# The opening work list of a local-convolution and maxout kernel, written anew

## The chip, the cores and the metric

The kernel runs on one core of one Trainium2 chip. The metric is the device time of one execution in microseconds (us). Engines are named as the profile names them: PE is TensorE, DVE VectorE, ACT ScalarE, POOL GpSimd, SP SyncE.

## The reference, cut to what matters

Each of 33280 positions (8 sequences of 4160) has 192 channels in 8 heads of 24. A softmax over 7 weights for each position and head mixes the position with the six before it. The result goes through three up matrices, an elementwise maximum of the three, and a down matrix.

```python
w = exp(weight_gen - max(weight_gen)); w = w / (sum(w) + 1e-9)   # over the 7 taps
x = einsum('bshk,bskhg->bshg', w, x_unf)                         # 7 taps, 8 heads of 24 channels
h = np.maximum(np.maximum(x @ w1, x @ w2), x @ w3)               # 192 -> 768
return (h @ w_out).astype(np.float32)                            # 768 -> 192
```

The up and down matrices come in as float64.

## The kernel before, in words

The positions are cut into 65 chunks of 512 (four tiles of 128). Chunk 0 is loaded alone, the later ones three at a time (a *super*: 0 is chunk 0, 1 is chunks 1 to 3, 2 is chunks 4 to 6). For each chunk the kernel does this:

- **softmax** (`softmax`, L207, once for a super, name `s`): a maximum over the taps on DVE (L212), a subtraction on POOL (L214), exp on ACT (L219), sum, addition and reciprocal on DVE (L221 to L223), a multiplication on POOL (L226).
- **products and sums** (`product`, L231, name `x<chunk>.<tile>`; `total`, L254, name `+`): POOL multiplies a tile's seven taps by the weights (L243), DVE adds the seven up (L258).
- **transpose** (`transpose`, L263, name `t`): channels onto partitions. For chunks 0 to 2 that is PE's work, two matmuls a tile into two PSUM tiles (L273, L274); later ones go through DVE's block transpose (L281) and 24 small copies on ACT (L287).
- **parts** (`parts`, L290, name `p`): the transposed values are split into a high and a low fp32r part: `xa_hi` on ACT (L297), `xa_lo` on DVE (POOL for chunk 3 and on, L301), `xc` and `xb` on ACT (L303, L305) and the lower half of `xb` on DVE or POOL (L306).
- **up** (`up`, L340): nine steps `(chunk, jp, i)`, where `jp` is a pair of 128-column blocks and `i` one of the three matrices. A step fills two PSUM tiles with nine matmuls for the upper and nine for the lower half of PE's rows; the second half of a step runs beside the first half of the next. `maximum` (L357) drains a tile: for `i = 0` a copy on ACT (L373), else a maximum on DVE (L375). After `i = 2` ACT rounds the result to `h_hi` (L378) and POOL makes `h_lo` (L382).
- **down** (`down`, L386): four groups of 24 matmuls, one a tile, drained by ACT (L405) and DVE (L406). Chunk c's stand in the middle of chunk c + 1, behind its sixth up step.

In the opening the weights have to be split too, from float64 words into fp32r high and low parts (`split`, L442). There are nine pieces `a0` to `a8`, one for each up step (step k of chunk 0 needs `a<k>`), three pieces `b0` to `b2` (one for every three steps) and six pieces `d0` to `d5` of the down matrix, all of which are needed before the down step of chunk 0. One piece has four stages: an absolute value on ACT (L458); a triple on DVE (L460, L462, L467); a rounding on ACT (L472) with a second triple on DVE (L474, L479, L483); and a scaling on ACT (L485) with a product on POOL (L486), which is the low part. A `b` piece has four more copies on ACT (L541). A piece holds one PSUM tile (a `b` piece two) from its first stage to its last.

All eight PSUM banks are one pool, named `ph`, for splits, transposes, up and down. Each engine takes its instructions in the order in which the program wrote them.

That order is written by ticks. A chunk has 22: two for an up step, four for the down groups. `OPENING` (L26) gives, for the first chunks, the stages written at each tick; each name there writes the next stage of that piece of work. `stage` (L569) first finishes what the named work needs: a `p` finishes its chunk's whole transpose, a `t` the sums, a sum its product. Work that `OPENING` doesn't name is written at the fixed ticks of `PRODUCTS`, `SUMS`, `TRANSPOSE`, `PARTS` and `SOFTMAX` (L85 to L89). The loop at L624 writes a tick's listed work ahead of that tick's matmuls; at the start of a chunk it finishes that chunk's `p`, and in chunk 0 the `a` and `b` of the step (L637 to L641), wherever the list has put them.

Of the kernel before, what the change touches and what calls it, by code (L numbers as in the profile page):

```python
# [24 lines left out]

OPENING = {  # L26
    -1: (
        "x0.0 s0 s0 x0.1 a0 a0 a0 a0 x0.2 +0.0 s0 x0.3 a2 a2 b0 +0.1 a1 b0 +0.2 b0 a3 a1 "
        "+0.3 s1 b0 a1 a2 s1 a1 s1 b0 a4 a2"
    ),  # L30
    0: "a6 b1 a6 a3 t0",
    1: "a6 a3 a5 a6 b1",
    2: "t0",
    3: "t0 a4 t0 a3 b1",
    4: "a5",
    5: "x1.0",
    6: "p0 b2 +1.0 x1.1",
    7: "s0 x1.2 a4 s1",
    8: "+1.1 t1",
    9: "a5 b2 a5 x1.3 b1",  # L40
    10: "b2 p0",
    11: "+1.2 b2 a4",
    12: "+1.3",
    13: "b1",
    15: "t1",
    16: "p0 a7 a8 a7 p1",
    17: "a7 d1",
    18: "t1 s2 a7 d1 a8",
    19: "p1 b2 a8",
    20: "d2 d2 d1",  # L50
    21: "d0",
    22: "d0",
    23: "d0",
    24: "+2.0 t1",
    25: "d2 +2.1 d1 p1",
    26: "d0 d3 d5",
    27: "d2 x2.1 d3",
    28: "d3 x2.2",
    29: "x2.0 x2.3 d3 d4 a8",
    31: "d4 s2 +2.2",  # L60
    32: "d5 d4 d5",
    33: "t2 +2.3 t2 t2",
    35: "d4 x3.2 p2",
    38: "p2 d5 p2 x3.0",
    42: "x3.1",
    43: "t3 t3",
    46: "t2 t3 +3.3 s2 +3.1 s2",
    48: "+3.2 +3.0",
    52: "x4.1 t3",
    56: "x4.0 p3",  # L70
    57: "p3 x3.3",
    59: "+4.1",
    60: "t3",
    61: "x4.2",
    66: "t3 x4.3",
    70: "t3",
    71: "p3",
    72: "+4.3 +4.2",
    74: "+4.0",
}  # L80


# [602 lines left out]
```

## Time and profile before

| | |
|---|---|
| time, median of 3 runs | 1723.65 us (1722.03 to 1723.68) |
| the profiled execution's time | 1720.92 us |
| its span, first to last instruction | 1719.1 us |
| mean granted TensorE clock | 0.996 |

Busy time of the span: PE 97%, POOL 83%, DVE 66%, ACT 66%. From the sixth chunk on, the first matmul of each chunk follows that of the chunk before by 25.35 us. The profile's line of 40 slices shows PE full from the third slice to the last but one.

Times in the views are us from the start of the span. A row of the timeline is: start, duration, engine, line, operation, output<-inputs, count, and in square brackets the engine's idle time just before it with what ended it. DVE's successive instructions overlap by some 0.1 us, so what one costs the queue is the distance to the next start.

### The profile page before, as it was taken

The page shows a single profiled execution, that of the slowest core. Times are in us where ns is not written, and L with a number is a line of the kernel's source. Part 1 is how long each engine was busy: PE and PEld are TensorE (multiplying, and loading weights), DVE is VectorE, ACT ScalarE, POOL GpSimd, SP SyncE. Part 2 cuts the span into 40 slices and gives each one's busy share as a digit, 9 for nine tenths or more (in the row PEclk, how much of TensorE's full clock was granted, in tenths as well). Part 3 has the DMA queues.
Part 4 walks back from the last instruction along what each step waited for, and adds up shares of the span by engine and source line. Part 5 has one row for each costly group of instructions (what it writes and reads, how often), then busy time and mean ns, then how long its engine had stood idle before and what let it go on. Part 6 is the DMA issues. An engine that isn't in the chain of part 4 may idle for free.

```text
span 1719.1 us, 42111 instructions
## 1 busy us (share of the span) xinstructions
PE 1671.4 (97%) x16794; PEld 1642.6 (96%) x16794; DVE 1136.5 (66%) x1570; ACT 1138.8 (66%) x2878; POOL 1427.9 (83%) x844
## 2 busy tenths in 40 slices
PE   2799999999999999999999999999999999999998
PEld 1589999999999999999999999999999999999998
DVE  7967666666666666666666666666666666666653
ACT  4556667667667667766766766766676676676662
POOL 5888888988888898888888898988889888888862
PEclk9999999999999999999999999999999999999999
DMA  7010101101010110101010110101011010101000
GB/s 233 1 69 10 69 20 60 69 20 59 20 70 10 69 48 32 69 20 69 11 70 20 60 69 19 60 20 69 17 63 69 20 60 20 69 11 45 20 11 29
DMA packets 19989, 79.50 MB, mean 46 GB/s; under 512 B 2272, under 2 KB 4568, under 8 KB 17104
## 3 DMA queue, kind: packets, MB, share of 16 engines
q1 hardware_dynamic: 19672, 76.54, 11.8%
q8 instruction: 131, 2.15, 0.5%
q14 instruction: 66, 0.54, 0.1%
q10 hardware_dynamic: 120, 0.28, 0.1%
HBM read 51.25 MB, written 25.56 MB: 45 GB/s over the span
## 4 chain that ended last, share of the span: by engine, by line
PE 92%; DVE 3%; POOL 2%; DMA 2%; issue 1%; SPq 0%; ACT 0%; POOLq 0%; ACTq 0%; DVEq 0%
PE ph L326 92%; DMA xt<-in_x_dram 1%; POOL r L243 1%; DVE acc L258 1%; DVE m L375 1%; POOL h_lo L382 1%; DMA h_lo<-in_moe_w_dram 0%; DVE e L483 0%; DVE ph L479 0%; DVE ph L462 0%; DVE ph L467 0%; DVE ph L474 0%; DVE ph L460 0%; POOL wt L226 0%; ACT wb_hi L541 0%
## 5 line engine op out<-in xcount | busy, mean ns | idle before, releaser
L243 POOL TENSOR_TENSOR r<-xt,wt 128x1344 f32<-128x1344 f32 x260 | 722.0, 2819 | 0.6 <-DMA h_hi<-in_moe_w_dram 0.6
L375 DVE TENSOR_TENSOR m<-ph,m 128x512 f32<-128x512 f32 x780 | 523.2, 685 | 217.9 <-PE ph L326 119.5
L382 POOL TENSOR_TENSOR h_lo<-m,h_hi 128x512 fp32r<-128x512 f32 x390 | 504.0, 1304 | 163.7 <-ACT h_hi L378 158.8
L326 PE MATMUL ph<-xa_hi,wa_hi 64*128 64x512 f32 x2340 | 626.8, 390 | 11.3 <-ACT xa_hi L297 4.4
L326 PE MATMUL ph<-xa_lo,wa_hi 64*128 64x512 f32 x2340 | 623.9, 388 | 2.8 <-DVE xa_lo L301 2.8
L326 PE MATMUL ph<-xa_hi,wa_lo 64*128 64x512 f32 x2340 | 623.3, 388 | 1.4 <-POOL wa_lo L486 1.3
L326 PE MATMUL ph<-xb,wb_hi 64*128 64x512 f32 x2340 | 623.0, 387 | 0.2 <-POOL xb L306 0.2
L326 PE MATMUL ph<-wo,h_hi 64*128 64x384 f32 x3120 | 597.0, 358 | 0.0
L326 PE MATMUL ph<-wo,h_lo 64*128 64x192 f32 x3120 | 554.9, 250 | 1.6 <-POOL h_lo L382 1.6
L378 ACT CAST h_hi<-m 128x512 fp32r<-128x512 f32 x390 | 241.9, 621 | 401.6 <-DVE m L375 398.6
L326 PEld LDWEIGHTS ph<-wo,h_hi 64*128 64x128 f32 x3120 | 486.1, 185 | 7.4 <-SPq L335 0.3
L326 PEld LDWEIGHTS ph<-wo,h_lo 64*128 64x128 f32 x3120 | 484.5, 188 | 2.2 <-POOL h_lo L382 2.1
L258 DVE TENSOR_REDUCE acc<-r 128x192 f32<-128x1344 f32 x260 | 401.9, 1547 | 109.1 <-POOL r L243 109.1
L287 ACT COPY room<-room 32x128 f32<-32x128 f32 x1488 | 440.7, 296 | 26.1 <-DVE room L281 7.9
L326 PE MATMUL ph<-xc,wb_lo 64*128 64x512 f32 x1170 | 453.2, 387 | 1.2 <-POOL wb_lo L486 1.2
L326 PEld LDWEIGHTS ph<-xa_hi,wa_hi 64*128 64x128 f32 x2340 | 364.2, 185 | 19.1 <-ACT m L373 5.9
L326 PEld LDWEIGHTS ph<-xa_hi,wa_lo 64*128 64x128 f32 x2340 | 357.5, 185 | 5.1 <-POOL wa_lo L486 3.0
L326 PEld LDWEIGHTS ph<-xa_lo,wa_hi 64*128 64x128 f32 x2340 | 357.0, 185 | 4.8 <-DVE xa_lo L301 3.3
L326 PEld LDWEIGHTS ph<-xb,wb_hi 64*128 64x128 f32 x2340 | 357.7, 185 | 2.8 <-POOL xb L306 0.7
L373 ACT COPY m<-ph 128x512 f32<-128x512 f32 x390 | 221.8, 585 | 56.3 <-PE ph L326 46.9
L406 DVE TENSOR_TENSOR o<-ph,ob 128x192 f32<-128x192 f32 x260 | 86.7, 353 | 240.4 <-ACT ob L405 240.4
L326 PEld LDWEIGHTS ph<-xc,wb_lo 64*128 64x128 f32 x1170 | 216.1, 185 | 3.0 <-POOL wb_lo L486 1.6
(57 smaller groups left out, 700.0 us busy)
## 6 DMA issues: line engine op xcount, KB each, us to landing
xt<-in_x_dram SPq DMA_DIRECT2D x20, 1728.0 KB, 7.0
out_dram<-o SPq DMA_DIRECT2D x65, 384.0 KB, 2.3
wt<-in_weight_gen_dram SPq DMA_DIRECT2D x21, 336.0 KB, 3.0
h_hi<-in_moe_w_dram SPq DMA_DIRECT2D x6, 256.0 KB, 5.0
xt<-in_x_dram SPq DMA_DIRECT2D x1, 1536.0 KB, 9.0
h_lo<-in_moe_w_dram SPq DMA_DIRECT2D x6, 192.0 KB, 5.5
room<-in_moe_w_out_dram SPq DMA_DIRECT2D x1, 1152.0 KB, 8.0
xt<-in_x_dram SPq DMA_DIRECT2D x1, 960.0 KB, 5.7
```

Source lines behind the costliest of these rows:

```text
L243: nc.gpsimd.tensor_tensor(r.rearrange("p (h g) k -> p k h g", g=G), xt[:, la + t : la + t + K].rearrange("p k (h g) -> p k h g", g=G), wt[ ...
L258: nc.vector.tensor_reduce(state["acc", c][:, t], r, axis=AX.X, op=ALU.add)
L287: pin(nc.scalar.copy(to[:, :, p : p + 32], blocks[p : p + 32, :, f : f + 32]))
L326: ins = nc.tensor.matmul(ph[:, :n], w[h], v[h], start=half == 0 and q == 0, stop=half == 1 and q == len(terms) - 1,)
L373: pin(nc.scalar.copy(m[:, :N], ph[:, :N]))
L375: pin(nc.vector.tensor_tensor(m[:, :N], ph[:, :N], m[:, :N], op=ALU.max))
L378: later(1, lambda: pin(nc.scalar.copy(hi, m[:, :N])))
L382: nc.gpsimd.tensor_tensor(lo, m[:, :N], hi.bitcast(F32), op=ALU.subtract)
L406: pin(nc.vector.tensor_tensor(o[:, t], po[:, :D], ob, op=ALU.add))
```

## The change: the diff

The list `OPENING` is replaced, and nothing else. Both lists lead to the same instructions on the same tiles; their order along each engine differs.

```diff
@@ -25,58 +25,59 @@
 
 OPENING = {
     -1: (
-        "x0.0 s0 s0 x0.1 a0 a0 a0 a0 x0.2 +0.0 s0 x0.3 a2 a2 b0 +0.1 a1 b0 +0.2 b0 a3 a1 "
-        "+0.3 s1 b0 a1 a2 s1 a1 s1 b0 a4 a2"
+        "s0 s0 s0 s0 x0.0 a0 a0 +0.0 a0 x0.1 x0.2 +0.1 a1 b0 x0.3 a1 b0 b0 +0.2 b0 p0 a2 "
+        "+0.3 s1 p0 a2 t0"
     ),
-    0: "a6 b1 a6 a3 t0",
-    1: "a6 a3 a5 a6 b1",
-    2: "t0",
-    3: "t0 a4 t0 a3 b1",
-    4: "a5",
-    5: "x1.0",
-    6: "p0 b2 +1.0 x1.1",
-    7: "s0 x1.2 a4 s1",
-    8: "+1.1 t1",
-    9: "a5 b2 a5 x1.3 b1",
-    10: "b2 p0",
-    11: "+1.2 b2 a4",
-    12: "+1.3",
-    13: "b1",
-    15: "t1",
-    16: "p0 a7 a8 a7 p1",
-    17: "a7 d1",
-    18: "t1 s2 a7 d1 a8",
-    19: "p1 b2 a8",
-    20: "d2 d2 d1",
-    21: "d0",
-    22: "d0",
-    23: "d0",
-    24: "+2.0 t1",
-    25: "d2 +2.1 d1 p1",
-    26: "d0 d3 d5",
-    27: "d2 x2.1 d3",
-    28: "d3 x2.2",
-    29: "x2.0 x2.3 d3 d4 a8",
-    31: "d4 s2 +2.2",
-    32: "d5 d4 d5",
-    33: "t2 +2.3 t2 t2",
-    35: "d4 x3.2 p2",
-    38: "p2 d5 p2 x3.0",
-    42: "x3.1",
-    43: "t3 t3",
-    46: "t2 t3 +3.3 s2 +3.1 s2",
-    48: "+3.2 +3.0",
-    52: "x4.1 t3",
-    56: "x4.0 p3",
-    57: "p3 x3.3",
+    0: "b0 a1 a3 t0 a3 t0",
+    2: "b1",
+    3: "a2 s1 a3 t0 b1",
+    4: "a1 a3 p0",
+    5: "b1 a5 a5 a2 s1 a6",
+    7: "a5 a4 b2 s1 x1.0 a4",
+    8: "a0 b1 a5 a4 b2 a4",
+    9: "a6 b2",
+    10: "x1.1 a6",
+    11: "a7 b2 a7 +1.1 a7 +1.0 a7 d0",
+    12: "b2 a8",
+    15: "a6 x1.2",
+    16: "a8 b1 x1.3",
+    18: "t1 d0",
+    19: "a8 a8 +1.2",
+    21: "+1.3 d0 d1 d1 x2.0 d3 t1 t1 p1 p1 d1 x2.1 d2 d2",
+    22: "d1 d0",
+    23: "p1 d4 d2",
+    24: "d2 d5",
+    25: "t1 d3 x2.2 d5",
+    27: "d4",
+    28: "d3 d5",
+    29: "d4 d3 +2.2 d5",
+    30: "d4",
+    31: "x2.3",
+    34: "+2.3",
+    36: "+2.1 p2 x3.1 t2 x3.0 s2 t2 t2 +2.0 t2 p2",
+    40: "+3.0",
+    41: "x3.2 +3.1",
+    46: "+3.2",
+    47: "+3.3",
+    48: "t3 s2",
+    50: "t3 s2 t3 p2",
+    51: "s2 x4.0",
+    55: "t3",
+    56: "+4.0 t3 t3",
+    57: "x3.3 x4.1 t3",
     59: "+4.1",
-    60: "t3",
-    61: "x4.2",
-    66: "t3 x4.3",
-    70: "t3",
-    71: "p3",
-    72: "+4.3 +4.2",
-    74: "+4.0",
+    61: "p3",
+    62: "p3",
+    63: "x4.2",
+    68: "+4.2",
+    69: "t4",
+    70: "p3 +4.3",
+    73: "t4 t4",
+    74: "t4",
+    78: "p4",
+    79: "t4",
+    80: "t4",
+    81: "p4 x4.3 p4 t4",
 }
```

Some of what it comes to, counted along both lists:

- Chunk 0's parts `p0`, and with them its transposes, are written ahead of `a2`, `a3`, `s1` and `b1` where before they stood behind the first triples of `a3` and `a6` and behind the sums of `s1`. `a0`'s scaling on ACT comes behind `p0`.
- `a6` goes from ticks 0 and 1 to ticks 5 to 15, `a4` and `a5` to ticks 5 to 8; `a7` comes at tick 11 instead of 16, `d0` at 11 to 21.
- Chunk 1's sums go from ticks 6 to 12 to ticks 11 to 21, its transposes from ticks 8 to 16 to ticks 18 to 21.
- Of chunk 2's sums, `+2.0` and `+2.1` go from ticks 24 and 25 to tick 36, behind the maxima of chunk 1's sixth step, with the softmax maximum of `s2`. All of chunk 2's transposes are written at tick 36, between the second and the third down group of chunk 0; before, three tiles' were written at tick 33 and the last at tick 35, ahead of the second group.
- Chunk 3's four sums, all at tick 43 before, are at ticks 40, 41, 46 and 47, and its transpose and parts some five ticks later. `p3`'s second POOL instruction comes ahead of the product `x4.3` instead of behind it.

## Rows read from the trace of the kernel before

**Rows 1.** The page, part 1: busy us of each engine over the span.
```profile
PE 1671.4 (97%) x16794; PEld 1642.6 (96%) x16794; DVE 1136.5 (66%) x1570; ACT 1138.8 (66%) x2878; POOL 1427.9 (83%) x844
```

**Rows 2.** Busy time by stretch; the first line names the columns.
```profile
core 0: us, PE busy (x) PEld busy (x) DVE busy (x) ACT busy (x) POOL busy (x), PEclk, DMA share, GB/s
24.00:60.00 36.00, 22.65 (x119) 14.22 (x119) 34.63 (x65) 19.71 (x45) 22.97 (x17) 0.97 0.31 114
60.00:91.00 31.00, 25.27 (x189) 18.20 (x190) 29.76 (x63) 15.12 (x37) 26.22 (x20) 0.93 0.00 1
88.03:101.68 13.65, 13.65 (x155) 13.14 (x152) 9.69 (x15) 6.07 (x13) 13.01 (x8) 1.00 0.01 2
101.68:154.32 52.64, 52.08 (x520) 47.11 (x517) 36.10 (x49) 35.29 (x89) 41.79 (x25) 1.00 0.15 57
300.00:400.00 100.00, 100.00 (x1017) 99.57 (x1014) 66.37 (x89) 67.67 (x174) 87.67 (x51) 1.00 0.10 39
```

**Rows 3.** Waits of PE from 24 to 140: total us, times, longest.
```profile
PE ph L326 <- ACT xa_hi L297: 4.4, 1, 4.4
PE ph L326 <- ACT m L373: 4.1, 3, 2.0
PE ph L273 <- DVE acc L258: 3.1, 3, 1.6
PE ph L326 <- ACT f L485: 1.7, 3, 0.9
```

**Rows 4.** Timeline of DVE, 13 to 25: a triple, sums and a softmax maximum.
```profile
13.23 0.42 DVE L460 TENSOR_SCALAR ph<-ph 128x256 f32<-128x256 f32 x1
...
14.50 1.54 DVE L258 TENSOR_REDUCE acc<-r 128x192 f32<-128x1344 f32 x1
17.08 0.57 DVE L460 TENSOR_SCALAR ph<-ph 128x384 f32<-128x384 f32 x1 [1.03 <-ACT ph L458]
...
23.00 1.55 DVE L258 TENSOR_REDUCE acc<-r 128x192 f32<-128x1344 f32 x1
24.46 0.84 DVE L212 TENSOR_REDUCE red<-wt 128x96 f32<-128x672 f32 x1
```

**Rows 5.** Timeline of DVE, 60 to 61 and 86 to 95.
```profile
60.71 0.84 DVE L212 TENSOR_REDUCE red<-wt 128x96 f32<-128x672 f32 x1
...
88.13 1.54 DVE L258 TENSOR_REDUCE acc<-r 128x192 f32<-128x1344 f32 x1
89.59 2.47 DVE L375 TENSOR_TENSOR m<-ph,m 128x512 f32<-128x512 f32 x4
```

**Rows 6.** Timeline of PE: last transposes, first matmuls, a wait, the third down group.
```profile
24.60 0.48 PE L273 MATMUL ph<-ident,acc 128*128 128x128 f32 x1 [1.12 <-DVE acc L258]
...
29.70 0.79 PE L326 MATMUL ph<-xa_hi,wa_hi 64*128 64x512 f32 x1 [4.41 <-ACT xa_hi L297]
33.33 0.79 PE L326 MATMUL ph<-xa_lo,wa_hi 64*128 64x512 f32 x1 [2.84 <-DVE xa_lo L301]
...
76.60 0.50 PE L326 MATMUL ph<-xa_hi,wa_hi 64*128 64x512 f32 x2 [2.00 <-ACT m L373]
...
92.07 0.41 PE L326 MATMUL ph<-wo,h_hi 64*128 64x384 f32 x2
```

**Rows 7.** Timeline of ACT, 36 to 41: a split's scaling, the second drain of step 0.
```profile
36.68 0.39 ACT L485 ACTIVATE f<-ph 128x256 f32<-128x256 uint32 x1 [0.95 <-DVE e L483]
...
40.95 0.59 ACT L373 COPY m<-ph 128x512 f32<-128x512 f32 x1 [1.51 <-PE ph L326]
```

**Rows 8.** Busy time around two waits of PE, columns as in rows 2.
```profile
56.00:66.00 10.00, 7.88 (x40) 5.24 (x42) 9.66 (x21) 5.64 (x14) 5.85 (x6) 0.66 0.00 0
74.00:76.00 2.00, 0.60 (x6) 0.17 (x2) 1.97 (x4) 1.01 (x5) 1.46 (x2) 1.00 0.00 0
```

**Rows 9.** Timeline of POOL, 124 to 133: chunk 4's last products, then chunk 3's parts.
```profile
124.76 5.41 POOL L243 TENSOR_TENSOR r<-xt,wt 128x1344 f32<-128x1344 f32 x2
130.25 1.28 POOL L306 TENSOR_TENSOR xb<-room,xc 64x512 fp32r<-64x512 f32 x1
```

## The prediction

> **What bounds the kernel now.** I read the busy shares first, then the same by stretch, then who PE waits for, then the timelines of the engines around those waits. Over the whole span PE is busy 97% [rows 1], and from chunk 5 on nothing but PE's own pace is left: 1017 matmuls in 100 us [rows 2]. A chunk has 258 (162 up, 96 down), so 25.4 us. All that the list can move lies ahead of that. Two stretches count. From 24 to 91 DVE is busy 34.63 of 36 us and 29.76 of 31, and what is missing is the few hundredths between instructions; PE's weight loads fill only 14.22 and 18.20 [rows 2]. PE is waiting for DVE there, directly or through ACT and POOL, and so the time at which DVE is through with the opening's work is the bound. From 88.03, where the down groups of chunk 0 begin, to 101.68, where chunk 2 begins (counted along PE's order), PE never stops (13.65 of 13.65). Then, from 101.68 to 154.32, two chunks take 52.64 us against 516 / 10.17 = 50.74 [rows 2]: 1.9 us are lost there. So a new list can earn something by letting PE come to the third down group earlier than 92.07 [rows 6], and at most 1.9 us behind it.
>
> **The top of the list.** Both lists reach the first `b` triple when its load has landed, at 17.08 [rows 4], with the same DVE work behind them except that `a2`'s first triple and `a1`'s trade places. From there the old list has one more triple ahead of the last sum of chunk 0: 14.50 - 13.23 = 1.27 us [rows 4]. So the new one ends that sum 1.27 earlier, and starts `s1`'s maximum at 24.46 - 1.27 = 23.19. The last transposes follow the sum, then ACT's copy, which now stands ahead of nearly all splits: some 0.6 us for each, so `xa_hi` at about 24.5, where before it ended at about 29.7 [rows 6]. But the third matmul needs `a0`'s low part, whose scaling ACT now has behind `a2`'s first stage, two copies for `xc`, two stages of `a1` and `a3`, and `xb`: seven instructions of 0.39 to 0.59 [rows 7], about 3.1 us, and 0.7 on POOL. That makes 28.4, and continuous matmuls from about 28.0 instead of 33.33 [rows 6]. PE leads by 5.3 us here.
>
> **Does the lead last?** Not if DVE is the bound. DVE has no less to do: I count along both lists what it must finish before PE can go from the second to the third down group of chunk 0, since chunk 2's transposes now stand there on PE and need `+2.0`, which is now the last of DVE's sums. Before, DVE's work from 24.46 to the last of the four maxima at 89.59 + 4 x 0.6 = 92.0 is 67.5 us [rows 4, 5]. The new order has the same instructions in it, plus `a2`'s first triple (1.27), minus `s2`'s maximum, which goes behind them (61.47 - 60.71 = 0.76, the 0.84 of the row less the overlap [rows 5]): 68.0. From 23.19 that ends at 91.2 if DVE never waits. Moving `+2.0` and `+2.1` (1.46 each, 88.13 to 89.59 [rows 5]) behind the maxima takes 2.9 us out of the path of the maxima but not out of this sum.
>
> **Waits that the new order adds on DVE.** First, `p0`'s subtraction is reached at 23.95 and its input comes at 24.5: 0.5. Second, `a5`'s first triple. Its absolute value stands on ACT behind step 0's second drain and `b1`'s rounding. That drain began 40.95 - 33.33 = 7.6 us after the matmuls got going [rows 6, 7]; so now at 35.6, and with 0.59 for the drain, 0.4 for the rounding and 0.4 for the absolute value [rows 7] DVE may start at 37.0. DVE gets there at 24.5 + 10.9 = 35.4 (two subtractions at 0.6 each, as a maximum of the same size, 2.47 / 4 [rows 5]; five `a` triples at 1.27; `b1`'s six instructions at 0.57 less the overlap, 3.3 [rows 4]): a wait of 1.6, with `s1`'s sums, `a4`, two maxima and much else queued behind it, and PE's next steps waiting for those. Third, chunk 1's first maxima, listed between the `d` triples: PE reaches chunk 1 late, because `a6`'s low part now comes from POOL only behind `a7`'s (tick 15), at about 57.8, and chunk 1's transposes stand ahead of the last matmuls of chunk 0 and wait for `+1.3`. I put 0.5 on that; nothing excludes 0, and 2 is the longest single wait of PE of this kind [rows 3]. Together 2.5 us, between 0.5 (the first alone) and 5 (all of them doubled). DVE then ends `+2.0` at 93.7, and with the last pair of transposes the third down group starts at 94.1 instead of 92.07: 2.0 late, between 0 and 4.5.
>
> **What else moves.** No transfer does: loads and stores stay where they were on SP, ACT and POOL issue none of those moved. SP's hand-overs between the two halves follow PE's own order. On POOL the products of chunks 1 and 2 go later; it has 22.97 of 36 and 26.22 of 31 us busy [rows 2], and the one that could bind is `x2.3`, now behind `d4`'s low part. `d4`'s second triple ends 9.6 us of DVE work ahead of `+2.0`'s end, at 84.1; with 0.9 for its last stage and 5.41 / 2 for the product [rows 9] `x2.3` is there at 87.7, and DVE asks for it at 87.4: 0.3, within the third wait, and up to 1 if POOL is late. Behind 92 DVE has 9.69 of 13.65 busy, then 36.10 of 52.64 [rows 2]: room for the 0.76 and for chunk 3's sums, which no longer stand in one clump of four ahead of chunk 1's last maxima. `p3`'s lower half no longer waits behind 5.41 us of products to 130.25 [rows 9], about when chunk 3's matmuls ask for it. Of the 1.9 us lost behind 101.68 I give back half, 1.0, between 0 and 1.9.
>
> **The sum.** +2.0 - 1.0 = +1.0 us, with ends of 0 - 1.9 = -1.9 and +4.5. It is made against the profiled execution, 1720.92 (span 1719.1 and 1.8 around it); that one is 2.7 under the median of the three runs, so on the median's scale it is 1723.65 + 1.0 = 1724.65, which I round to 1724.7.
>
> **Rivals.** *PSUM was the bound (faster).* PE waited 4.1 us for ACT's drains and 1.7 for ACT's last split stage [rows 3]: those are waits for a free `ph` tile. Along the old list up to eight tiles are held when another is asked for, along the new one at most seven. If those 5.8 us are what holds PE up, they go: 1717.9. The Trainium skill (Perfetto Trace Analysis, Optimization Strategy) has it that the same gap coming back on the engine that should be full can mean that no PSUM is left for the next tile; by that rule this rival would be the likeliest. Against it: DVE has no idle time in that stretch [rows 2], and the drains that PE waits for stand behind DVE's triples on ACT. 0.11.
>
> *TensorE's clock falls in the new wait (slower).* Place: PE ahead of chunk 2's transposes, with two down groups done. By the lead above it gets there at about 90, and waits 3 to 4 us for `+2.0`. In 56 to 66 the granted clock averaged 0.66, which is 6.8 us at 1.2 GHz instead of 2.4, after a stretch with many waits; in 74 to 76 it stayed at 1.00 through a wait of 2.00 [rows 6, 8]. Behind the third group PE is the bound, so the half rate would not be hidden: 6.8 / 2 = 3.4 us on top of +1.0, 1728.1. It decides from the moment that the clock reads 0.50 there; with a wait twice as long as the one that left the clock alone I give it, together with more DVE waits than 4 us, 0.32. The Trainium skill (TensorE: Matmul & The Clock Gate, HAM oscillation) says that a wait for data that is long enough sets the PE back to the throttled rate and the next work starts cold. By that rule the time would be 1728.1.
>
> *It does nothing to the path.* DVE waits as little as before, PE comes to the third group at 92.1 to 92.5, and half of the 1.9 comes back: 1722.9. The new order of the same work then just shows in other places. 0.20.
>
> **How the numbers follow.** About 0.2% (3.4 us) is what a measurement of this kernel can tell from no change. The forecast (+1.0, own range 1721.7 to 1727) has 0.37 and lies within it, as does the rival that nothing happens, 0.20: same 0.57. Faster is the PSUM rival, 0.11; slower the clock with the long waits, 0.32. The range goes from 1720.5 (all of the 1.9 back and DVE without waits, less 1.2 for the spread of the runs) to 1729.5 (the clock's 1728.1 and 1.4 of further waits); what it leaves out is the PSUM rival and the worst of the slow end, 0.2.
>
> **What would show it.** Right: the first `xa_hi` at about 24.5 and steady matmuls from 28; an idle DVE of 1 to 2 us near 36; the last sum of chunk 2 ending at 92 to 95; PE idle for some us just ahead of chunk 2's transposes; the third down group at 93 to 96; fewer losses between there and chunk 4. Wrong: that group starting at 90 or earlier, or DVE idle by more than 6 us between 24 and 92, or matmuls at half rate behind 94.

## The result, and the profile after

The changed kernel takes 1726.81 us (median of 10 runs, 1724.46 to 1729.33), the kernel before 1722.49 us beside it (10 runs, 1720.45 to 1723.68): a ratio of 1.0026 with a 95% interval of 1.0016 to 1.0036, 2.8 to 6.2 us slower. The time lies in the stated range, but beyond the 0.2% that the forecast allowed around 1724.7 us (+1.0). What came is the slower rival's mechanism: a wait ahead of chunk 2's transposes, with TensorE's clock falling in it. Of the ten executions four have a mean granted clock of 0.992 and take 1724.5 to 1726.4 us, six have 0.989 or 0.990 and take 1726.5 to 1729.3 us; the traced one (1725.62 us) is one of the four.

The busy shares say nothing of it. The changed list is one line longer, so that L327 of the views below is L326 of the kernel before, and so on. Part 1 of the page of the changed kernel, beside [rows 1]:

```profile
PE 1675.3 (97%) x16794; PEld 1653.3 (96%) x16794; DVE 1135.9 (66%) x1570; ACT 1138.4 (66%) x2878; POOL 1428.0 (83%) x844
```

Busy time by stretch, columns as in [rows 2], the changed kernel. The third and the fifth row are the counterparts of the third and fourth there (chunk 0's first down group to chunk 2, and chunks 2 and 3); the fourth is a piece of the third:

```profile
24.00:60.00 36.00, 22.51 (x116) 15.41 (x117) 33.52 (x71) 20.59 (x49) 20.68 (x18) 0.86 0.32 115
60.00:91.00 31.00, 26.08 (x199) 19.85 (x197) 27.84 (x57) 14.48 (x36) 25.58 (x20) 0.89 0.00 1
85.63:106.55 20.92, 16.16 (x159) 15.39 (x160) 13.80 (x18) 7.82 (x16) 19.12 (x10) 0.92 0.00 1
94.00:97.50 3.50, 3.24 (x18) 2.78 (x20) 1.56 (x3) 1.49 (x3) 3.50 (x3) 0.54 0.02 5
106.55:157.22 50.67, 50.67 (x519) 50.53 (x516) 35.82 (x48) 35.79 (x90) 41.44 (x25) 1.00 0.15 59
300.00:400.00 100.00, 100.00 (x1016) 99.67 (x1015) 64.18 (x87) 67.55 (x172) 87.48 (x51) 1.00 0.10 38
```

The stretch from the first down group to chunk 2, which PE filled before (13.65 of 13.65 us [rows 2]), now lasts 20.92 us with PE busy for 16.16, part of it at a granted clock of 0.54. Chunks 2 and 3 take 50.67 us where they took 52.64, and they now leave PE no gap. Who PE waits for from 24 to 140, beside [rows 3]:

```profile
PE ph L327 <- ACT f L486: 7.0, 2, 3.9
PE ph L327 <- POOL wa_lo L487: 5.8, 4, 2.3
PE ph L274 <- DVE acc L259: 4.8, 1, 4.8
```

The last row is one wait of 4.8 us of a transpose (L274) for a sum (L259). The kernel before has three waits of this kind, all for tiles of chunks 0 and 1 and none over 1.6 us [rows 3]; new are the length and the place, between the second and the third down group of chunk 0:

```profile
85.63 0.41 PE L327 MATMUL ph<-wo,h_hi 64*128 64x384 f32 x1 [0.25 <-DVE m L376]
...
89.11 0.39 PE L327 MATMUL ph<-wo,h_lo 64*128 64x192 f32 x2
94.26 0.42 PE L274 MATMUL ph<-ident,acc 128*128 128x128 f32 x1 [4.76 <-DVE acc L259]
94.47 0.42 PE L275 MATMUL ph<-ident,acc 128*64 128x128 f32 x1
...
95.75 0.42 PE L275 MATMUL ph<-ident,acc 128*64 128x128 f32 x1
96.10 0.69 PE L327 MATMUL ph<-wo,h_hi 64*128 64x384 f32 x2
96.59 0.36 PE L327 MATMUL ph<-wo,h_lo 64*128 64x192 f32 x2
...
97.66 0.29 PE L327 MATMUL ph<-wo,h_lo 64*128 64x192 f32 x2
97.79 0.35 PE L327 MATMUL ph<-wo,h_hi 64*128 64x384 f32 x2
97.98 0.25 PE L327 MATMUL ph<-wo,h_lo 64*128 64x192 f32 x2
```

Two down groups are done at 89.5. Then all eight transposes, not the last pair alone, come behind the wait, 0.21 us apart, and the third group starts at 96.10 (before: 92.07 [rows 6]). From one `h_lo` matmul of a down group to the next it is 0.53 us up to 97.66 and some 0.3 from there on: half rate, then full. The prediction had named half rate behind 94 as a sign of being wrong, and 93 to 96 for the third group. What PE waited for, in DVE's timeline:

```profile
23.19 0.84 DVE L213 TENSOR_REDUCE red<-wt 128x96 f32<-128x672 f32 x1
24.46 0.69 DVE L302 TENSOR_TENSOR xa_lo<-ph,xa_hi 128x512 fp32r<-128x512 f32 x1 [0.43 <-ACT xa_hi L298]
...
35.49 0.56 DVE L484 TENSOR_SCALAR e<-ph 128x384 uint32<-128x384 uint32 x1 [0.39 <-ACT hi L473]
...
87.25 0.69 DVE L376 TENSOR_TENSOR m<-ph,m 128x512 f32<-128x512 f32 x1 [1.17 <-ACT m L374]
...
91.11 3.00 DVE L259 TENSOR_REDUCE acc<-r 128x192 f32<-128x1344 f32 x2
94.03 0.84 DVE L213 TENSOR_REDUCE red<-wt 128x96 f32<-128x672 f32 x1
```

`+2.1` and `+2.0` are the two sums at 91.11; the second ends at 94.1.

Read along PE's order, the trace of one profiled execution of each kernel gives these starts, in us, where "down" is chunk 0's first down group and "third" its third. The experiments are told below; the ratios are to the kernel before, run in the same session.

| | first matmul | chunk 1 | down | third | chunk 2 | chunk 4 | ratio, interval |
|---|---|---|---|---|---|---|---|
| before | 29.70 | 69.34 | 88.03 | 92.07 | 101.68 | 154.32 | |
| changed | 24.48 | 71.65 | 85.63 | 96.10 | 106.55 | 157.22 | 1.0026 [1.0016, 1.0036] |
| 1 transposes later | 24.26 | 71.48 | 85.98 | 89.61 | 100.56 | 151.19 | 0.9987 [0.9978, 0.9996] |
| 2 sums back | 24.21 | 71.42 | 88.23 | 93.08 | 102.77 | 153.40 | 0.9990 [0.9982, 0.9999] |
| 3 old list, late sums | 30.09 | 70.62 | 85.11 | 98.23 | 108.52 | 160.99 | 1.0021 [1.0012, 1.0029] |
| 4 old list, new end | 29.78 | 69.42 | 88.95 | 92.96 | 102.57 | 153.20 | 0.9987 [0.9978, 0.9995] |
| 5 old top, rest of 1 | 30.11 | 69.76 | 84.23 | 94.16 | 105.60 | 156.28 | 1.0002 [0.9993, 1.0011] |
| 6 last tiles last | 24.43 | 71.62 | 85.61 | 94.71 | 105.77 | 156.44 | 1.0011 [1.0002, 1.0020] |
| 7 `a6` first | 24.68 | 72.69 | 86.22 | 96.72 | 108.43 | 159.14 | 1.0026 [1.0015, 1.0036] |
| 8 all sums late | 23.95 | 72.58 | 86.68 | 90.17 | 105.11 | 156.63 | 1.0000 [0.9991, 1.0009] |
| 9 old top, early `d` | 30.50 | 71.86 | 85.86 | 89.49 | 100.32 | 150.99 | 0.9977 [0.9968, 0.9986] |
| 10 = 1, again | 24.27 | 71.34 | 85.71 | 89.33 | 100.26 | 150.93 | 0.9988 [0.9979, 0.9997] |

The changed kernel's lead of 5.2 us at the first matmul is a lag of 2.3 at chunk 1, a lead of 2.4 at the down step (two sums were taken from in front of it), a lag of 4.0 at the third group, 4.9 at chunk 2 and 2.9 at chunk 4.

### The profile page after: what moved, and what is told of

It is laid out like the page before. It is cut to its first block, busy times and chain, and to the rows that moved or that the text cites. A ratio compares the mean times of both kernels' runs of the same rounds, so it can differ in the third digit from the quotient of the medians.

```text
span 1723.8 us, 42110 instructions
## 1 busy us (share of the span) xinstructions
PE 1675.3 (97%) x16794; PEld 1653.3 (96%) x16794; DVE 1135.9 (66%) x1570; ACT 1138.4 (66%) x2878; POOL 1428.0 (83%) x844
## 4 chain that ended last, share of the span: by engine, by line
PE 95%; DVE 3%; DMA 1%; ACT 1%; issue 0%; SPq 0%; POOL 0%; POOLq 0%; DVEq 0%; ACTq 0%
PE ph L327 95%; DVE acc L259 1%; DVE m L376 0%; DMA h_lo<-in_moe_w_dram 0%; DVE e L484 0%; DVE ph L480 0%; DVE ph L463 0%; DVE ph L475 0%; DVE ph L468 0%; DMA xt<-in_x_dram 0%; DVE ph L461 0%; SPq L518 0%; ACT ph L459 0%; ACT f L486 0%; PE ph L274 0%
## 5 line engine op out<-in xcount | busy, mean ns | idle before, releaser
L327 PE MATMUL ph<-xa_hi,wa_hi 64*128 64x512 f32 x2340 | 628.6, 391 | 10.9 <-ACT f L486 7.0
L327 PE MATMUL ph<-xa_hi,wa_lo 64*128 64x512 f32 x2340 | 625.3, 389 | 5.8 <-POOL wa_lo L487 5.8
L327 PE MATMUL ph<-xa_lo,wa_hi 64*128 64x512 f32 x2340 | 625.0, 388 | 0.0
L327 PE MATMUL ph<-xb,wb_hi 64*128 64x512 f32 x2340 | 624.3, 388 | 0.0
L327 PE MATMUL ph<-wo,h_hi 64*128 64x384 f32 x3120 | 597.9, 360 | 0.2 <-DVE m L376 0.2
L327 PE MATMUL ph<-wo,h_lo 64*128 64x192 f32 x3120 | 556.6, 250 | 1.6 <-POOL h_lo L383 1.6
L327 PEld LDWEIGHTS ph<-wo,h_hi 64*128 64x128 f32 x3120 | 488.6, 185 | 6.5 <-issue 1.0
L327 PEld LDWEIGHTS ph<-wo,h_lo 64*128 64x128 f32 x3120 | 487.1, 189 | 2.1 <-POOL h_lo L383 2.1
L259 DVE TENSOR_REDUCE acc<-r 128x192 f32<-128x1344 f32 x260 | 401.7, 1546 | 111.7 <-POOL r L244 111.7
L327 PE MATMUL ph<-xc,wb_lo 64*128 64x512 f32 x1170 | 453.6, 388 | 0.0
L327 PEld LDWEIGHTS ph<-xa_hi,wa_hi 64*128 64x128 f32 x2340 | 366.3, 185 | 15.3 <-ACT f L486 8.2
L327 PEld LDWEIGHTS ph<-xa_hi,wa_lo 64*128 64x128 f32 x2340 | 358.6, 185 | 9.3 <-POOL wa_lo L487 7.9
L327 PEld LDWEIGHTS ph<-xa_lo,wa_hi 64*128 64x128 f32 x2340 | 359.0, 185 | 1.8 <-DVE xa_lo L302 0.4
L327 PEld LDWEIGHTS ph<-xb,wb_hi 64*128 64x128 f32 x2340 | 358.7, 185 | 1.4
L327 PEld LDWEIGHTS ph<-xc,wb_lo 64*128 64x128 f32 x1170 | 216.6, 185 | 1.2 <-issue 0.2
```

The lines of the kernel that those rows point to most:

```text
L259: nc.vector.tensor_reduce(state["acc", c][:, t], r, axis=AX.X, op=ALU.add)
L327: ins = nc.tensor.matmul(ph[:, :n], w[h], v[h], start=half == 0 and q == 0, stop=half == 1 and q == len(terms) - 1,)
```

## The experiments

Theory A is throughout that DVE sets the time of the opening, and that the changed kernel loses its time where PE, in order, waits at chunk 2's transposes for DVE's last sum. Theory B is the rival that each expectation names.

**1. Chunk 2's transposes later.** The changed kernel with them behind the third and fourth down group:

```diff
-    36: "+2.1 p2 x3.1 t2 x3.0 s2 t2 t2 +2.0 t2 p2",
-    40: "+3.0",
-    41: "x3.2 +3.1",
+    36: "+2.1 x3.1 x3.0 s2 +2.0",
+    40: "t2 t2 t2 t2 p2 p2 +3.0",
+    41: "p2 x3.2 +3.1",
...
-    50: "t3 s2 t3 p2",
+    50: "t3 s2 t3",
```

> The changed kernel with chunk 2's transposes and parts written at ticks 40 and 41, behind all four down groups of chunk 0, instead of at tick 36 between the second and the third; its late sums stay late. Theory A (the loss is PE's wait of 4.8 us there for the last sum): the third down group starts at about 89 to 90 instead of 96.1, PE fills the wait with down groups and chunk 1's steps, chunk 2 starts at 99 to 101 instead of 106.55, and the time is 5 to 7 us under the changed kernel, 1 to 4 us under the kernel before. Theory B (the top of the list, with a6 and chunk 1's sums late, costs the time, and the wait only shows it): the wait turns up again at the next place that needs DVE, chunk 2 starts at 104 or later, and the time is at most 2.5 us under the changed kernel.

1719.89 us against 1721.68, ratio 0.9987; the changed kernel's was 1.0026. This is what A said, in time and in the trace. Busy time from the first down group to chunk 2, and two rows of PE's timeline:

```profile
85.98:100.56 14.58, 14.56 (x159) 13.30 (x160) 12.54 (x16) 7.50 (x16) 14.58 (x9) 1.00 0.01 2
```

```profile
95.28 0.33 PE L274 MATMUL ph<-ident,acc 128*128 128x128 f32 x1
95.45 0.27 PE L275 MATMUL ph<-ident,acc 128*64 128x128 f32 x1
```

DVE ends `+2.0` at 95.2, no earlier than in the changed kernel, and PE doesn't care: it has two down groups and some matmuls of an up step to do, the clock stays at 1.00, and chunk 2 starts 6.0 us earlier. Moving eight transposes in PE's queue, with the parts that follow them, takes the whole loss away.

**2. The two sums back.** The changed kernel with `+2.0` and `+2.1` at ticks 24 and 25 again:

```diff
-    24: "d2 d5",
-    25: "t1 d3 x2.2 d5",
+    24: "+2.0 d2 d5",
+    25: "+2.1 t1 d3 x2.2 d5",
...
-    36: "+2.1 p2 x3.1 t2 x3.0 s2 t2 t2 +2.0 t2 p2",
+    36: "p2 x3.1 t2 x3.0 s2 t2 t2 t2 p2",
```

> The changed kernel with chunk 2's sums +2.0 and +2.1 back at ticks 24 and 25, ahead of the maxima of chunk 1's steps; the transposes stay at tick 36. Theory A: no wait ahead of the transposes, but the maxima come 2.9 us later, so that the first down group starts at 88 to 89 instead of 85.6 and the third at 92 to 94 instead of 96.1: 2 to 4 us under the changed kernel, 0 to 2 us over the kernel before. Theory B: within 1 us of the changed kernel.

Ratio 0.9990: 0.0036, or 6.2 us, under the changed kernel, where A had 2 to 4, and 1.7 us under the kernel before, where A had 0 to 2 over it. The down step comes at 88.23, 2.6 later than in the changed kernel and 0.2 later than before, and the transposes, now without a wait, put the third group 1.0 behind that of before. A had these starts right; it had not counted that what chunks 2 and 3 win back (they take 50.63 here, 52.64 before) stays. At chunk 4 its trace is 3.8 us ahead of the changed kernel's and 0.9 ahead of that of before; the rest of the differences in time it doesn't show there.

**3. The old list with late sums.** The kernel before with `+2.0`, `+2.1` and all of chunk 2's transposes at tick 36:

```diff
-    24: "+2.0 t1",
-    25: "d2 +2.1 d1 p1",
+    24: "x2.0 t1",
+    25: "d2 x2.1 d1 p1",
...
-    33: "t2 +2.3 t2 t2",
-    35: "d4 x3.2 p2",
+    33: "+2.3",
+    35: "d4 x3.2",
+    36: "+2.1 +2.0 p2",
```

> The kernel before with one part of the change alone: +2.0 and +2.1 behind chunk 1's maxima at tick 36, and chunk 2's transposes there, between the second and the third down group. Theory A: DVE's work still ends at about 92, all eight transposes follow it, the first down group starts 1 to 2 us earlier than 88.0 and the third at 93.5 to 95 instead of 92.1: 1.5 to 3 us over the kernel before. Theory B: within 0.5 us of the kernel before, as the top of the list is the old one.

Ratio 1.0021, 3.6 us, a little over A's figure and far from B's. But the trace doesn't show A's wait at its size. PE's timeline:

```profile
87.78 0.44 PE L327 MATMUL ph<-wo,h_hi 64*128 64x384 f32 x1 [1.60 <-POOL wo L487]
...
90.79 0.69 PE L327 MATMUL ph<-wo,h_hi 64*128 64x384 f32 x1 [2.28 <-POOL wo L487]
...
96.36 0.45 PE L274 MATMUL ph<-ident,acc 128*128 128x128 f32 x1 [0.97 <-DVE acc L259]
```

The down step, 2.9 us earlier than before, waits 3.9 us for the last pieces of the down matrix (`wo`, L487 on POOL), which the old list finishes at ticks 35 to 38. The wait for the sum is 0.97, and the granted clock in 85 to 98 is 0.67. So in this run what the early maxima won goes to the late pieces, and it doesn't show what the late sum alone would cost with the old top.

**4. The old list with the new end.** The kernel before up to chunk 2's parts, and the new list's order for the work of chunks 3 and 4 (`x3.1 x3.0` at tick 36, `+3.0` to `+3.3` at 40 to 47, and the rest of the diff from there).

> The kernel before with the changed kernel's order from tick 36 on for the products, sums, transposes and parts of chunks 3 and 4. If that order is what wins back 2.0 us between chunk 2 and chunk 4: 1.3 to 1.9 us under the kernel before, chunk 2 taking 25.3 to 25.8 us instead of 26.57. If the 2.0 us came back only because PE was late and the other engines had caught up: within 0.5 us of the kernel before.

Ratio 0.9987. Up to tick 34 the two lists are the same; the down step is 0.9 us later here all the same, and so is chunk 2 (101.68 there, 102.57 here), so far apart are two executions of the same order. Chunks 2 and 3 take 50.63 us:

```profile
102.57:153.20 50.63, 50.63 (x518) 48.73 (x516) 35.33 (x47) 35.16 (x89) 42.47 (x26) 1.00 0.15 59
```

PE is busy in all of it. So the first of the two outcomes came: the gain behind chunk 2 belongs to that end of the list and does not need a late start.

**5. The old top with the rest of 1.** The list of before up to tick 35 (without the early `+2.0`, `+2.1` and `t2`) and its `d5` at 38, the first experiment from tick 36 on.

> The list of before for chunk 0 and the opening's splits (first xa_hi at 29.7, as before), with chunk 2's sums +2.0 and +2.1 late, its transposes behind the third down group as in the first experiment, and the new order for chunks 3 and 4. It asks whether the new top of the list is worth anything. Theory A (DVE's work bounds the opening, so an earlier first matmul is not kept): chunk 0's down step starts at 85 to 86.5, chunk 2 at 100 to 101.5, the time is within 1 us of the first experiment's. Theory B (the start 5 us earlier is kept, at least in part): 2 to 5 us over the first experiment.

Ratio 1.0002, 0.0015 over the first experiment, as B had it, but not for B's reason. Who PE waits for, from 84 to 108:

```profile
PE ph L335 <- POOL wo L495: 3.9, 2, 2.3
```

The down step starts at 84.23, earlier than with the new top, and meets the same late down-matrix pieces as in 3; from there PE runs at half rate for a while (granted clock 0.78 in 84 to 92, 0.73 in 92 to 98). Experiment 9 takes that fault out.

**6. The last tiles last.** In the changed kernel `+2.0` and `+2.1` change places with `+2.2` and `+2.3`:

```diff
-    29: "d4 d3 +2.2 d5",
+    29: "d4 d3 +2.0 d5",
...
-    34: "+2.3",
-    36: "+2.1 p2 x3.1 t2 x3.0 s2 t2 t2 +2.0 t2 p2",
+    34: "+2.1",
+    36: "+2.2 p2 x3.1 t2 x3.0 s2 t2 t2 +2.3 t2 p2",
```

> The changed kernel with one exchange: the sums of chunk 2's tiles 0 and 1 are written at ticks 29 and 34, those of tiles 2 and 3 at tick 36, where the changed kernel has it the other way round. PE transposes the tiles in the order 0 to 3 and the sum that comes last belongs now to tile 3. Theory A (what the prediction had at 0.4 us, the last pair of transposes behind the last sum, was all eight because the first tile was the last to be summed): PE does up to six transposes ahead of the last sum, the third down group starts 0.4 to 1.0 behind the end of that sum where it was 2.0, at 94.5 to 95.2 in place of 96.1, and the time is 1 to 2 us under the changed kernel. Theory B (the order of the tiles doesn't matter, since PE waits for the same sum): within 0.5 us of it.

Ratio 1.0011, 0.0015 or 2.6 us under the changed kernel, a little over A's figure. PE's timeline:

```profile
89.42 0.33 PE L274 MATMUL ph<-ident,acc 128*128 128x128 f32 x1
...
92.69 0.33 PE L274 MATMUL ph<-ident,acc 128*128 128x128 f32 x1 [2.62 <-DVE acc L259]
92.86 0.27 PE L275 MATMUL ph<-ident,acc 128*64 128x128 f32 x1
94.15 0.41 PE L274 MATMUL ph<-ident,acc 128*128 128x128 f32 x1 [1.02 <-DVE acc L259]
94.36 0.42 PE L275 MATMUL ph<-ident,acc 128*64 128x128 f32 x1
94.71 0.69 PE L327 MATMUL ph<-wo,h_hi 64*128 64x384 f32 x2
```

Two tiles are transposed at once, the third behind its own sum, the last pair 0.6 us ahead of the third group, at 94.71. The wait stays and so does the half rate. Of the profiled execution's 1.4 us at the third group 0.8 are left at chunk 2, since the half rate falls on more of the down matmuls.

**7. `a6` ahead of `a7`.** The changed kernel with `a6`'s last stage at the head of tick 11, in place of tick 15.

> The changed kernel with the last stage of the split a6 written ahead of those of a7 (tick 11 instead of 15). Step 6 of chunk 0 no longer waits for a7's scaling on ACT and product on POOL. Theory A (DVE's work sets when chunk 2's last sum is through, and that ends PE's wait): step 6 starts 1 to 2 us earlier than 55.65, the third down group at 95.5 to 96.3 all the same, time within 1 us of the changed kernel. Theory B (the waits of PE for late splits in chunk 0 are what the time was lost to): 2 to 4 us under it.

Ratio 1.0026, the changed kernel's own. Step 6 of chunk 0 starts at 52.45 where it had started at 55.65, and nothing of these 3.2 us reaches chunk 1 (72.69, which is later) or the third group (96.72, where A had 95.5 to 96.3). The wait for the last sum is as long as it was:

```profile
94.85 0.45 PE L274 MATMUL ph<-ident,acc 128*128 128x128 f32 x1 [4.75 <-DVE acc L259]
```

B's 2 to 4 us don't come. The run shortens one of PE's waits for late splits and not the sum of its waits, which is 17.5 us from 24 to 84 here and 16.7 in the changed kernel.

**8. All four sums late.** As 1, with `+2.2` and `+2.3` at tick 36 too, `s2` at 37 and the transposes at 41.

> As the first experiment (chunk 2's transposes behind the third down group), and all four of chunk 2's sums behind the maxima of chunk 1's sixth step, where it has two of them ahead. Theory A (DVE bounds PE up to the down step of chunk 0, and what is taken from DVE ahead of the maxima is won there as long as the transposes have time): the two sums are 2.9 us; chunk 0's down step starts at 83.5 to 85.5 where the first experiment had 85.98, chunk 2 at 99 to 100.5, time 0 to 1.5 us under the first experiment. Theory B (PE then only comes earlier to the transposes and waits there for the sums): chunk 2 at 100.5 or later, and the time equal to the first experiment's or above it.

Ratio 1.0000, 0.0013 over 1, and chunk 2 at 105.11. A's numbers are wrong here, and B's come without its reason, since PE is not earlier at the transposes. POOL's timeline and, below it, DVE's:

```profile
85.34 0.60 POOL L488 TENSOR_TENSOR wo<-f,e 128x192 fp32r<-128x192 f32 x1 [1.13 <-ACT f L487]
91.35 2.80 POOL L245 TENSOR_TENSOR r<-xt,wt 128x1344 f32<-128x1344 f32 x1 [5.41 <-DVE acc L260]
```

```profile
94.19 3.01 DVE L260 TENSOR_REDUCE acc<-r 128x192 f32<-128x1344 f32 x2 [1.52 <-POOL r L245]
...
101.87 1.55 DVE L260 TENSOR_REDUCE acc<-r 128x192 f32<-128x1344 f32 x1 [2.85 <-POOL r L245]
103.34 0.68 DVE L303 TENSOR_TENSOR xa_lo<-ph,xa_hi 128x512 fp32r<-128x512 f32 x1
```

A sum gives a product's buffer back (`r` has three). With all sums late three products of chunk 2 hold them, the fourth can't start before the first sum, POOL stands for 5.41 us, and DVE waits for that product and, at 101.87, for the next (`x3.0`). That second wait reaches PE by the edit itself: with the transposes at tick 41, `+3.0` of tick 40 stands ahead of `p2`'s subtraction on DVE, in 1 it stands behind. PE waits 2.4 us for that subtraction and 1.2 at the transposes. So the stopped producer is shown, and what it alone costs is not. The maxima did end 1.8 us earlier than in 1 (89.7 against 91.5), but the down step started 0.7 later, as chunk 1 had started 1.1 later; up to there the two lists are the same, so the 1.1 is a difference between executions.

**9. The old top with early `d` pieces.** Experiment 5 with `d3`, `d4`, `d5` moved up:

```diff
-    22: "d0",
-    23: "d0",
...
-    38: "d5",
+    22: "d0 d3",
+    23: "d0 d5",
+    24: "x2.0 t1 d1 d3",
+    25: "d2 x2.1 p1 d5",
+    26: "d0 d2 d3 x2.2 d4",
+    27: "d5 d3",
+    28: "d4 d5",
+    29: "d4 +2.2",
+    30: "d4",
+    31: "x2.3 s2",
+    34: "+2.3",
```

> The fifth experiment with its one fault mended: the list of before for the top, chunk 2's transposes behind the third down group and the new order behind them, and the pieces d3, d4 and d5 of the down matrix finished about as early as in the changed kernel (d5 by tick 28 in place of 38, d4 by tick 30 in place of 35), the product x2.3 behind them. In the fifth experiment PE waited 3.9 us for their last POOL stage. Theory A (that wait was what the fifth experiment lost; the earlier start of the new top is worth nothing): the wait goes, the third down group starts at 88.5 to 90.5 where the fifth had 94.16, chunk 2 at 99.5 to 101.5, and the time is within 1 us of the first experiment's, run again beside it. Theory B (the new top is worth 2 us or more): 2 to 4 us over the first experiment's.

1718.17 us against 1721.88, ratio 0.9977 [0.9968, 0.9986]: the fastest kernel here, ahead of the kernel before and of the changed one. From the first down group to chunk 2 and over chunks 2 and 3:

```profile
85.86:100.32 14.46, 14.46 (x158) 13.53 (x160) 11.75 (x15) 8.07 (x17) 14.15 (x8) 1.00 0.01 2
100.32:150.99 50.67, 50.67 (x518) 49.51 (x516) 36.93 (x50) 34.92 (x89) 44.22 (x26) 1.00 0.15 59
```

No gap is left from the down step on. The first matmul starts 6.2 us later than in 10, and chunk 2 starts at 100.32 against 100.26. Theory A holds where it was asked: the new top is worth nothing at chunk 2. PE waits as long ahead of it in both, 17.7 us from 24 to 104 here and 17.4 in 10, only in other places: for ACT's last split stage 1.8 here and 7.0 there. By time the kernel is even below A's 1 us (0.0011, 1.9 us, under 10), but the two intervals overlap.

**10. Experiment 1 again.**

> The first experiment once more, as the measure for the ninth and for how far a ratio repeats between sessions: 0.9978 to 0.9996 of the kernel before, chunk 2 at 100.0 to 101.1. A ratio of 1.0 or more would mean that its gain was a matter of the session.

Ratio 0.9988 against 0.9987, chunk 2 at 100.26 against 100.56: it repeats.

## Where the prediction was right and where it was wrong, point by point

- **The top: right.** `s1`'s maximum at 23.19 (predicted 23.19), first matmul 24.48 (24.5), third matmul 28.31 (28.4).
- **The lead doesn't last: right.** DVE ends the last sum at 94.1 (93.7); experiments 7 and 9 show it from both sides: a step 3.2 us earlier puts the third group 0.6 later, and a start 6.2 us later than in 10 puts it 0.2 later.
- **DVE's waits: right in sum, not in place.** From `s1`'s maximum to the end of that sum it takes 70.9 us, of which 2.7 are its waits (2.5 predicted) and 68.2 its work (68.0). The 1.6 ahead of `a5` didn't come (a wait of 0.39 just ahead of it did), and 1.17 came at a maximum of chunk 1, ahead of 87.25.
- **The step that failed: "with the last pair of transposes the third down group starts at 94.1".** The last sum is that of tile 0, whose transposes are the first in PE's order, so all eight waited. They take 2.0 us from the sum to the third group where the prediction had 0.4. Of these 1.6 us some 0.9 are the clock (eight transposes 0.11 us apart take 0.9 in experiment 1, 0.21 apart 1.8 here), the rest the order: in experiment 6, with the last pair alone behind its sum, it is 0.6 from the sum to the third group, at half rate.
- **The clock: the rival's mechanism, at half its price.** The prediction put PE at the wait at 90, for 3 to 4 us; it was 89.5 and 4.76. Half rate cost 0.9 in the transposes and 0.8 in the down matmuls up to 97.66 (third group to chunk 2: 10.45 us, before 9.61), 1.7 us in all, not 3.4. The forecast had counted the wait and left the clock at 1.00, with a row for a wait of 2.00 us [rows 6, 8] and none for one of 3 to 4. By the Trainium skill (TensorE: Matmul & The Clock Gate, HAM oscillation) the work behind a long wait starts cold, and here the trace agrees: 0.54 in 94 to 97.5. That the rival's total of +4.4 us is so near the measured +4.3 is luck in part: it had the clock too dear by 1.7 and what comes back behind chunk 2 too small by 1.0, and up to chunk 4 the trace shows 2.9.
- **Behind chunk 2: right in sign, too small.** 1.97 us came back, all there was, not 1.0; experiment 4 shows that the end of the list does it by itself.
- **The sum.** At the third group the loss is 0.4 (DVE) and 1.6 over the +2.0; 0.8 of clock follow, 1.97 come back. That makes 4.03 + 0.84 - 1.97 = 2.9 us at chunk 4. The profiled spans differ by 4.7. Of the other 1.8 the last section says what is known; the interval of 2.8 to 6.2 us holds both figures. What the untraced executions add to the median is open.
- **PSUM was the bound: fell.** PE's wait for the last split stage rose from 1.7 to 7.0 us where fewer tiles are held, and experiments 9 and 10 reach chunk 2 together with 1.8 and 7.0. The rule of the Trainium skill (Perfetto Trace Analysis, Optimization Strategy) that a returning gap can mean no PSUM is left would have led to the wrong cause here.
- **Nothing on the path: fell**, by a wait of 4.76 us that is not there before.

What stays open: experiments 1, 2 and 4 have ratios of 0.9987 to 0.9990, though their profiled executions reach chunk 4 at 151.19, 153.40 and 153.20. With executions of the same order 0.9 and 1.1 us apart (experiments 4 and 8) and the ends that the last section shows, one traced execution is no finer than some 2 us here. The third group's 4.0 us and chunk 2's 4.9 are clear of that; the terms of the sum above that are under 1 us are read from one trace each.

## What to carry to other kernels

Work that an in-order engine must wait for should stand in its queue behind work that it can already do, and what is finished last should be consumed last: the same late sum cost nothing with two down groups ahead of the transposes. A lead of one engine is worth counting only at the next point where the engine that sets the pace is asked; here 5 to 6 us at the first matmul were nothing at chunk 2. Before a consumer of a buffer is put off, count the buffers: two late sums cost nothing, four stopped the producer for 5.41 us.

## What the runs showed of the hardware that was not expected

What stood ahead of a fall of TensorE's clock: in the changed kernel PE waits 4.76 us, and the transposes behind it run at half rate (0.21 us apart). In experiment 6 two transposes stand inside that stretch: those behind a first wait of 2.62 us run at full rate (0.17 us apart), those behind a further 1.02 at half (0.21).

The last chunk's length differs between two executions of one kernel: from its first matmul to its last down matmul 39.37 us in experiment 1, 40.70 in its repetition. The stretch from 1704 to 1709 of the two, in that order:

```profile
1704.00:1709.00 5.00, 5.00 (x58) 5.00 (x56) 0.36 (x1) 0.64 (x2) 0.00 (x0) 0.76 0.01 3
```

```profile
1704.00:1709.00 5.00, 5.00 (x40) 5.00 (x40) 0.36 (x1) 0.32 (x1) 0.00 (x0) 0.50 0.01 3
```

PE is full in both, at a granted clock of 0.76 and 0.50. The pace of the chunks between differs as well, 25.3525 and 25.3595 us each, 0.4 us over 59 chunks. The changed kernel's profiled execution had the longer of both (40.77 and 25.360), the kernel before the shorter (39.37 and 25.353): that is the 1.8 us by which the spans differ more than chunk 4's start. All twelve traces have the same two waits of PE in the last chunk, of about 0.91 and 0.68 us; nine take 39.34 to 39.45 us for that chunk, two 40.70 and 40.77, and experiment 8, whose granted clock stays at 1.00 in it, 37.88. What decides between them no run here shows.
